# Value units ahead of logits, later x parts, own tiles for raw output weights, and VectorE remainders behind two sums, in a gated mix of attention and SwiGLU

## The chip, the cores and the metric

The kernel runs on one core of one Trainium2 chip. The metric is the device time of one execution in microseconds (us), lower is better. The engines are named as the profile names them: PE is TensorE's matmul, PEld its weight load, DVE is VectorE, ACT is ScalarE, POOL is GpSimd, SP is SyncE, which issues the DMAs.

## The reference

The input x has 2048 tokens of width 576. One branch is an attention with 32 heads of width 18 over four segments of 512 tokens with a memory carried from segment to segment; the other is a SwiGLU network of width 4608. A gate mixes the two.

```python
for s in range(N):                                    # N = 4 segments of L = 512
    qs, ks, vs = q[:, :, s], k[:, :, s], v[:, :, s]
    logits = jnp.einsum("bhqd,bhkd->bhqk", qs, ks) * scale + mask
    p = _softmax(logits, axis=-1)
    a_dot = jnp.einsum("bhqk,bhkd->bhqd", p, vs)
    pq = phi(qs)
    num = jnp.einsum("bhld,bhde->bhle", pq, M)
    den = jnp.einsum("bhld,bhd->bhl", pq, z)[..., None] + 1e-6
    outs.append(g * (num / den) + (1.0 - g) * a_dot)
    M = M + jnp.einsum("bhld,bhle->bhde", phi(ks), vs)
    z = z + jnp.einsum("bhld->bhd", phi(ks))
a = concat_heads(outs) @ wo
b = (_silu(x @ w_gate) * (x @ w_up)) @ w_down
out = sigmoid((x * gate_w).sum(-1)) * a + (1 - that gate) * b
```

The mask adds -1e9 where the key lies behind the query in the segment. Products with x, wq, wk, wv, wo, w_gate, w_up and w_down are in fp32.

## The kernel before

**Number format.** Most products are made from a high and a low half of each operand. The high half is a ScalarE copy, rounded; the low half is the remainder that VectorE subtracts (`low`, L271; `split_by`, L963; `split`, L137). Each product then takes hi·hi, hi·lo and lo·hi.

**First phase, up to about 220 us.** For each of the four segments the kernel makes queries and keys (`qk`), values (`v_step`, matmuls at L159), the update of the memory, and `mem_step` (L460), which reads the memory for 128 tokens and half of the heads. It runs 24 times, one call behind each value step of the segments 1 to 3, and takes PSUM banks 3, 4 and 2 in turn.

**Second phase, about 217 to 1635 us.** The hidden width is cut into 36 features of 128. The tokens are cut into two halves; features 0 to 35 in the text are those of the first half, 36 to 71 of the second. Gate and up projection of a feature are made together for two segments, with a scheme of seven products in place of eight (as Strassen's). `seven(t, j)` is product j, 0 to 6: six matmuls of 128x128 by 512 at L1018 and one at L1021 for the last 64 input rows. Products accumulate into three PSUM banks a, y and xx, with copies and sums between them: y = a + p5 (VectorE, L1087) must be done before product 5 adds to it; xx = copy of a (ScalarE, L1094) before product 6 adds to it; the sum p5 = a + p5 (VectorE, L1095) is used only in the closing multiplications (L1103, L1104). With q the number of the feature modulo 3, the features with q=0 also run the down projection of the three features before, in groups of nine matmuls (L868) whose results VectorE adds to `ya` (L876, L878).

**What sets the order.** The order in which the Python code calls the engines is the order in each engine's queue; the waits between engines follow from the tiles. Each feature has eight beats, k = 0 to 7, called between the products (`tick`, `beat`). A beat first issues what was deferred to it (`due`), then down groups, then, by a credit, a step of attention. Deferred are the preparation of the next feature's weights (`w_make`: sums on GpSimd, L264; high halves on ScalarE, L268; low halves on VectorE, L271; at the beats of the tables HIGH and LOW), the halves of the hidden values (`split_by`, L962 and L963) and of the down weights, and the loads. By these tables the low halves for products 4, 5 and 6 come up at the beats k = 1, 2 and 3 of the feature that uses them.

**Attention** is a generator, `att_gen`. Its step tau is the n-th, 0 to 5, of a unit of six. In a step with n from 0 to 4 it makes logits (`s_bank`, L726, into a bank that `ts_tile` gives), one step later the row maxima (VectorE, L732) and exponentials (ScalarE, L744), three steps later the cast to two 16-bit halves (L758 on VectorE, L759 on GpSimd), and four steps later the transposing DMA (SP, L763). After six steps a value unit is due (`v_unit`, matmuls at L774 and L775, a reduce at L781). `ts_tile` has banks 5 and 6 while down groups are pending, and one more rule: directly after a new set of groups came (`fed`), bank 7.

**The break.** Between features 35 and 36 ten beats (919 to 945 us) run the last 16 down groups' work and make the x operands of the second half (`x_second`): loads, sums on GpSimd and splits (L136 on ScalarE, L137 on VectorE), each at a beat that the tables LOADS, SUMS and PARTS name as (beat, z, j). **The end**: from feature 71 on the weights of the output projection are loaded (`wo_load`, L910) into the ring `raw` that also holds the feature weights, split (L913, L914), and used in a tail from about 1635 us on.

Of the kernel before, what the change touches and what calls it, by code (L numbers as in the profile page):

```python
# [12 lines left out]
F32 = mybir.dt.float32  # L13
# [7 lines left out]
P = 128  # L21
S = 2048
D = 576
# [4 lines left out]
FT = 36  # L28
# [4 lines left out]
NT = 5  # L33
HR = [(128 * t // DH, -(-min(128 * t + 128, D) // DH)) for t in range(NT)]
MW = max(b - a for a, b in HR) * E
CH = 3
# [12 lines left out]
SHARE = (0, 0, 2, 2, 3, 3, 3, 3)  # L49
BREAK = 10  # L50
LOADS = ((-3, 0, 0), (-2, 0, 1), (3, 1, 0), (4, 1, 3), (4, 0, 3), (5, 0, 2), (5, 1, 1), (6, 1, 2))
SUMS = ((2, 0, 1), (9, 0, 4), (10, 0, 2), (10, 1, 1), (11, 1, 4), (12, 0, 6), (12, 1, 2), (13, 1, 6))
PARTS = ((1, 0, 0), (4, 0, 1), (10, 1, 0), (10, 0, 5), (11, 0, 3), (11, 1, 5), (12, 1, 3), (13, 0, 4), (14, 0, 2),
         (14, 1, 1), (15, 1, 4), (16, 1, 2), (17, 0, 6), (18, 1, 6))
FIRST = (9, 10, 11, 15, 17, 17, 19)
SLOT = (0, 3, 2, 1, 4, 6, 5)
RPOS = (0, 1, 4, 2, 5, 6, 3)
# [4 lines left out]
def f32(ap):  # L62
    return ap.bitcast(F32)
# [3 lines left out]
def gated_mix(ctx, tc, xT, xrest, wf, wfr, wfh, wd, wv, wo, beta, cmask, ident, bmask, out):  # L67
    nc = tc.nc
# [44 lines left out]
    taken = {}  # L113
    clock = [0]
    fed = []
# [6 lines left out]

    def ts_tile(shape=(P, L)):
        ids = (5, 6) if groups else (5, 6, 7, 3, 4)
        if fed and groups[0][0] < FT // CH - 1 and max(taken, key=taken.get) != 7:
            ids = (7,)
        fed.clear()
        return ps.tile(list(shape), F32, name=f"bank{soonest(ids, HELD)}")

    def group_tile(shape=(P, L)):  # L130
        return ps.tile(list(shape), F32, name=f"bank{soonest((3, 4, 7), 1)}")

    groups = []

    def split(hi, lo, src):
        nc.scalar.activation(hi, src, AF.Copy)  # L136
# [79 lines left out]
    def raw_tile():  # L216
        return rp.tile([P, L], F32, name="raw")
# [14 lines left out]
    def op_tile():  # L232
        return wop.tile([P, 2, 2, P], F32R, name="wo_")
# [22 lines left out]
    def w_make(half, f, LOW=LOW):  # L256
        g, u = wraw_of.pop(f)
        ops = wops[half, f] = [None] * 7
        a11, a12, a21, a22 = g[:, 0:2], g[:, 2:4], u[:, 0:2], u[:, 2:4]
        src = [a11, None, None, a12, None, None, a22]  # L260

        def total(j, p, q, sub=True):
            src[j] = rp.tile([P, 2, P], F32, name="ws", bufs=3)
            (nc.gpsimd.tensor_sub if sub else nc.gpsimd.tensor_add)(src[j], p(), q())  # L264

        def high(j):
            ops[j] = op_tile()
            nc.scalar.activation(ops[j][:, 0], src[j], AF.Copy)  # L268

        def low(j):  # L270
            nc.vector.tensor_sub(ops[j][:, 1], src[j], f32(ops[j][:, 0]))  # L271

        def keep(j):
            nc.sync.dma_start(wc[f, j], f32(ops[j]).rearrange("p a k n -> p (a k n)"))

        todo = [(LEAD - 2, lambda: total(1, lambda: a21, lambda: a22, False)),
                (LEAD - 1, lambda: total(2, lambda: src[1], lambda: a11)),
                (LEAD + 2, lambda: total(4, lambda: a11, lambda: a21)),
                (LEAD + 4, lambda: total(5, lambda: a12, lambda: src[2]))]
        for j in range(7):  # L280
            todo += [(HIGH[j], lambda j=j: high(j)), (LOW[j], lambda j=j: low(j))]
            if half == 0 and f < KEPT:
                todo.append((LEAD + j + 3, lambda j=j: keep(j)))
        return sorted(todo, key=lambda t: t[0])
# [3 lines left out]
    with ExitStack() as st:  # L288
# [310 lines left out]
        for s in range(NSEG):  # L599
# [58 lines left out]
            for n in range(8):  # L658
                hf, i = divmod(n, 4)
                flush()  # L660
                v_step(s, hf, i)
                if s:
                    mem_step(s, n // 2, n % 2)
                if s < 3:
                    if n == 0:
                        xs_of[s + 1] = x_tiles(s + 1)
                    if 1 <= n < 6:
                        x_split(xs_of[s + 1], n - 1, raws["x", n - 1])
                else:
                    if n == 4:  # L670
                        wraw_of[1] = [w_load(1, u) for u in range(2)]
                    if n < 2:
                        first_sum(6, n)
                    elif n < 6:
                        if n < 4:
                            nc.gpsimd.memset(f32(rhs[n - 2][96:]), 0.0)
                        if 3 <= n < 5:
                            r_fetch(n - 3)
                    if n > 2:
                        for z in stack_loads(0)[2 * n - 6:2 * n - 4]:  # L680
                            nc.sync.dma_start(*z)
# [8 lines left out]
    with ExitStack() as st:  # L690
        cps = []
        due = deque()

        def defer(k, fn):
            while len(due) < k:
                due.append([])
            due[k - 1].append(fn)

        rw = pool(st, "rw", 4)
        fp = pool(st, "fp", CH)  # L700
# [97 lines left out]
        def att_gen():  # L798
            N = 12 * NB

            def at(t):
                return 5 * (t // 6) + t % 6 if 0 <= t < N and t % 6 < 5 else None

            held = []
            for tau in range(N + 10):
                u, n = divmod(tau, 6)
                if n == 2 and sends:
                    nc.sync.dma_start(*sends.pop(0))
                if 1 <= n <= 3 and u + 1 < 2 * NB:
                    for d in stack_loads(u + 1)[3 * n - 3:3 * n]:  # L810
                        nc.sync.dma_start(*d)
                if n == 2 and u > 1 and u % 2 == 1 and (u - 3) // 2 < NB:
                    o_step((u - 3) // 2)
                z = at(tau - PL)
                if z is not None:
                    p_bank(z)
                z = at(tau - 1)
                if z is not None:
                    e_bank(z)
                if n == 5 and 1 <= u <= 2 * NB:  # L820
                    held.append(u)
                if held and (groups or n == 0):
                    v = held.pop()
                    v_unit(v - 1)
                    if v % 4 == 1 and v // 4 + 1 < 4 * NSEG:
                        v_fetch(v // 4 + 1)
                z = at(tau)
                if z is not None:
                    s_bank(z)
                z = at(tau - XL)  # L830
                if z is not None:
                    x_bank(z)
                yield
            for z in sends:
                nc.sync.dma_start(*z)
# [10 lines left out]
        def d_fetch(f):  # L846
            d = d_tile()
            nc.sync.dma_start(f32(d).rearrange("p a n -> p (a n)"), dc[f])
            return d
# [50 lines left out]
        def gates():  # L900
            nc.vector.tensor_scalar_add(gg, gg, 1.0)
            nc.vector.reciprocal(gg, gg)
            nc.vector.tensor_scalar(g1, gg, -1.0, 1.0, op0=OP.mult, op1=OP.add)

        def wo_load(n, hf, c):
            box = []

            def load():
                box.append(raw_tile()[:, :96 * NT].rearrange("p (k n) -> p k n", n=96))
                nc.sync.dma_start(box[0], wo[:, :, 288 * hf + c.start:288 * hf + c.stop])  # L910

            defer(n, load)
            defer(n + 5, lambda: nc.scalar.activation(wos[hf][:, 0, :, c], box[0], AF.Copy))  # L913
            defer(n + 7, lambda: nc.vector.tensor_sub(wos[hf][:, 1, :, c], box[0], f32(wos[hf][:, 0, :, c])))  # L914
# [45 lines left out]

        def split_by(k, hi, lo, src):
            defer(k, lambda: nc.scalar.activation(hi, src, AF.Copy))  # L962
            defer(k + 1, lambda: nc.vector.tensor_sub(lo, src, f32(hi)))  # L963

        def beat(k=None, half=0):
            for fn in due.popleft() if due else ():
# [57 lines left out]
        draw = {}  # L1024
# [4 lines left out]
        for pos, (half, f) in enumerate(seq):  # L1029
# [27 lines left out]
            def tick():  # L1057
                k = step[0]
                step[0] += 1
                if k % 2 == 0 and f and stores:  # L1060
                    nc.sync.dma_start(*stores.pop(0))
                if half == 0:
                    if (q, k) in ((0, 3), (1, 3), (2, 2)):
                        draw[f] = d_load(f)
                    if (q, k) in ((1, 1), (1, 7), (2, 4)):
                        g = f - 1 if k == 1 else f
                        ds[half, g] = d_split(g, draw.pop(g))
                elif (q, k) in ((1, 0), (1, 2), (2, 1)):
                    g = f - 1 if k == 0 else f
                    ds[half, g] = d_fetch(g)  # L1070
                beat(k, half)

            ops, rem = wops.pop((half, f)), rhs[f % 2]
            hh = fp.tile([P, 2, L], F32R, name="hh")
# [10 lines left out]
            seven(a, 2, False)  # L1085
            y = y_tile()
            nc.vector.tensor_add(y, a, p5)  # L1087
            tick()
            seven(xx, 3, False)
            nc.scalar.activation(sg0, xx, AF.Copy)  # L1090
# [2 lines left out]
            xx = x_tile()  # L1093
            nc.scalar.activation(xx, a, AF.Copy)  # L1094
            nc.vector.tensor_add(p5, a, p5)  # L1095
            tick()
            nc.scalar.activation(sg0, sg0, AF.Silu)  # L1097
            seven(y, 5, False)
# [33 lines left out]
        ops = None  # L1132
# [6 lines left out]
        for n in range(17):  # L1139
# [24 lines left out]
            ops = nxt  # L1164
# [54 lines left out]
```

## Time and profile before

| | us |
|---|---|
| median of three runs (lowest to highest) | 1724.15 (1723.75 to 1724.97) |
| the profiled execution, its own time | 1724.43 |
| its span, first to last instruction | 1722.7 |
| TensorE busy | 1706.5 |
| VectorE busy | 1359.8 |
| ScalarE busy | 1084.8 |
| GpSimd busy | 938.4 |

The span is what lies between the first and the last instruction of the profiled execution; the rest of its time lies around it. A busy time counts an engine's instructions, and pipelined matmuls overlap: a row's length is longer than the distance to the next. In a timeline each row has a start, a length, the engine, the line, the operation, the tiles written and read, and a count for a run of like instructions; a bracket at its end gives the idle time before and what ended it. Granted clock was 1.000 of full speed.

### The profile page before, as it was taken

How to read it: one execution, taken by the hardware profiler on the slowest of the kernel's cores; microseconds unless marked ns; L12 is line 12 of the kernel's file. 1: busy time of each engine (PE TensorE's matmuls, PEld its weight loads, DVE VectorE, ACT ScalarE, POOL GpSimd, SP SyncE). 2: the span in 40 equal slices, each digit the busy share in tenths (PEclk: the TensorE clock that was granted, in tenths of full speed). 3: DMA queues.
4: the chain of work that ended last, by engine and by line, in shares of the span. 5: the costliest groups of instructions: out<-in, count | busy, mean ns of one | idle time of the engine just before them, and what ended most of it. 6: DMA issues, size and time to landing. Idle time of an engine off the chain costs nothing.

```text
span 1722.7 us, 34832 instructions
## 1 busy us (share of the span) xinstructions
PE 1706.5 (99%) x11868; PEld 1481.0 (86%) x11868; DVE 1359.8 (79%) x3231; ACT 1084.8 (63%) x2123; POOL 938.4 (54%) x1194
## 2 busy tenths in 40 slices
PE   9999999999999999999999999999999999999999
PEld 7899978888888888888887888888888888888899
DVE  6557588898899889898989677788887778778655
ACT  7666585776677577667765755765666576566411
POOL 4434646666666656565666555555555555555221
PEclk9999999999999999999999999999999999999999
DMA  8654499999998898988879986887778677767544
GB/s 284 233 186 153 151 311 191 232 226 186 209 227 192 181 215 200 193 198 203 210 144 256 290 177 133 178 186 162 148 181 182 147 157 185 163 132 167 165 144 137
DMA packets 524002, 328.05 MB, mean 190 GB/s; under 512 B 411184, under 2 KB 460336, under 8 KB 523824
## 3 DMA queue, kind: packets, MB, share of 16 engines
q1 hardware_dynamic: 523824, 325.83, 77.5%
q8 instruction: 93, 1.52, 0.4%
q14 instruction: 85, 0.70, 0.1%
HBM read 165.76 MB, written 76.09 MB: 140 GB/s over the span
## 4 chain that ended last, share of the span: by engine, by line
PE 83%; DVE 6%; ACT 5%; DMA 3%; issue 2%; POOL 1%; SPq 1%; DVEq 0%; ACTq 0%; POOLq 0%
PE bank L1018 33%; PE bank L868 24%; PE bank L159 10%; PE bank L1021 5%; PE bank L726 4%; PE bank L774 2%; PE bank L775 1%; PE bank L414 1%; ACT pe L744 1%; ACT L744 1%; PE bank L460 1%; DVE xo L137 1%; DVE p L758 1%; DVE scr L732 1%; PE bank L350 1%
## 5 line engine op out<-in xcount | busy, mean ns | idle before, releaser
L759 POOL TENSOR_TENSOR p<-pe,p 128x512 f16<-128x512 f32 x320 | 376.0, 1175 | 420.4 <-DVE p L758 406.2
L868 PE MATMUL bank<-dw,hh 128*128 128x320 f32 (+1 forms) x2304 | 489.0, 305 | 2.8 <-DVE ya L878 2.8
L868 PEld LDWEIGHTS bank<-dw,hh 128*128 128x128 f32 x2304 | 381.4, 190 | 14.4 <-DVE ya L878 3.8
L744 ACT ACTIVATE pe<-bank,mb 128x512 f32<-128x512 f32 (+3 forms) x512 | 247.9, 526 | 197.7 <-DVE mb L732 191.3
L868 PE MATMUL bank<-dw,hl 128*128 128x320 f32 (+1 forms) x1152 | 340.6, 296 | 0.2 <-DVE hl L137 0.2
L732 DVE CUSTOM_DVE_ANT_0 scr<-bank,cm 128x512 bf16<-128x512 f32 (+3 forms) x512 | 246.6, 482 | 6.8 <-PE bank L726 0.2
L878 DVE TENSOR_TENSOR ya<-bank,ya 128x320 f32<-128x320 f32 x352 | 158.3, 453 | 83.9 <-PE bank L868 83.2
L868 PEld LDWEIGHTS bank<-dw,hl 128*128 128x128 f32 x1152 | 218.0, 189 | 0.4 <-DVE hl L137 0.4
L1021 PE MATMUL bank<-xr,rh 128*128 128x512 f32 x504 | 196.5, 390 | 0.0
L752 POOL TENSOR_SCALAR_AFFINE_SELECT pe<-pe 128x256 f32<-128x256 f32 (+1 forms) x320 | 149.8, 469 | 54.1 <-ACT pe L744 51.0
L758 DVE CAST p<-pe 128x512 f16<-128x512 f32 x320 | 152.5, 477 | 0.0
L264 POOL TENSOR_TENSOR ws<-raw 128x256 f32<-128x256 f32 x140 | 118.3, 845 | 17.4 <-DMA raw<-in_wf_dram 4.5
L726 PE MATMUL bank<-kst,qst 108*128 108x512 bf16 (+3 forms) x512 | 125.2, 306 | 2.1 <-ACT pe L744 2.1
L1021 PEld LDWEIGHTS bank<-xr,rh 128*128 128x128 f32 x504 | 94.7, 188 | 20.3
L963 DVE TENSOR_TENSOR hl<-row,hh 128x512 fp32r<-128x512 f32 x120 | 104.2, 868 | 8.3 <-ACT hh L962 7.8
L1095 DVE TENSOR_TENSOR row<-bank,row 128x512 f32<-128x512 f32 x72 | 49.7, 690 | 64.7 <-ACT bank L1094 64.5
L744 ACT ACT_TABLE_LOAD x69 | 88.5, 1283 | 11.1 <-DVE mb L732 10.1
L1080 ACT ACTIVATE bank<-bank 128x512 f32<-128x512 f32 x72 | 41.9, 582 | 80.5 <-PE bank L1021 77.4
L1090 ACT ACTIVATE row<-bank 128x512 f32<-128x512 f32 x72 | 43.3, 601 | 78.0 <-PE bank L1021 77.8
L1097 ACT ACT_TABLE_LOAD x71 | 91.1, 1283 | 1.3
L264 POOL TENSOR_TENSOR ws<-raw,ws 128x256 f32<-128x256 f32 x70 | 58.3, 833 | 49.4 <-DVE wo__22504 L271 10.9
L159 PE MATMUL bank<-xo,qhi 128*128 128x512 f32 x264 | 83.2, 396 | 0.4 <-ACT vps L399 0.4
(2166 smaller groups left out, 4097.9 us busy)
## 6 DMA issues: line engine op xcount, KB each, us to landing
raw<-in_wf_dram SPq DMA_DIRECT2D x140, 256.0 KB
rh<-rc SPq DMA_DIRECT2D x72, 336.0 KB
dc<-dw SPq DMA_DIRECT2D x36, 576.0 KB
dw<-dc SPq DMA_DIRECT2D x36, 576.0 KB
stk<-q SPq DMA_DIRECT2D x32, 384.0 KB
draw<-in_wd_dram SPq DMA_DIRECT2D x36, 288.0 KB
rc<-rt SPq DMA_DIRECT2D x42, 224.0 KB
vd<-vps SPq DMA_DIRECT2D x8, 912.0 KB
```

The source lines that it names most:

```text
L159: nc.tensor.matmul(t, st[n], mv[n], start=(n == 0), stop=(n == 13))
L264: (nc.gpsimd.tensor_sub if sub else nc.gpsimd.tensor_add)(src[j], p(), q())
L726: nc.tensor.matmul(t[:, c:c + w], qs[:KR, pr, P * i:P * i + P], ks[:KR, pr, 0:w], start=True, stop=True)
L732: nc.vector.tensor_tensor_reduce(scr[:, :w], t[:, c:c + w], cm[:, L - w:L], -SCALE, 3.0e38, OP.add, OP.min, m[:, k:k + 1])
L744: nc.scalar.activation(pe[:, c:c + w], t[:, c:c + w], AF.Exp, bias=m[:, k:k + 1], scale=SCALE)
L752: nc.gpsimd.affine_select(d, d, pattern=pat, compare_op=OP.is_ge, fill=0.0, base=0, channel_multiplier=1)
L758: nc.vector.tensor_copy(p[:, 0], pe)
L759: nc.gpsimd.tensor_sub(p[:, 1], pe, p[:, 0])
L868: nc.tensor.matmul(ts[m], p, q[:, cs], start=(n == 0), stop=(n == 3 * CH - 1))
L878: nc.vector.tensor_add(ya[:, i, cs], t, ya[:, i, cs])
L1018: nc.tensor.matmul(t, w[:, p, z], x[z][:, q], start=first and n == 0, stop=False, skip_group_check=True)
L1021: nc.tensor.matmul(t, rem[:, RPOS[j]], XR[j], start=False, stop=True, skip_group_check=True)
```

## The change

There are six edits.

1. A value unit that is due is always issued in a step with n = 0, which has logits directly behind it. Before, it was issued at the next step whenever down groups were pending.
2. `ts_tile`'s rule for bank 7 applies to the logits alone, and no longer to the value unit's bank.
3. `mem_step` is called twice behind every second value step, not once behind each.
4. The x operands of the second half are split in another order and at later beats; three splits and one sum move behind the ten beats of the break, into feature 36.
5. The raw output weights have other tiles in three places: two of their own (`wr`) and the one of `draw`, which is free by then.
6. VectorE remainders (`low` and that of `split_by`) that come up in the beats k=1 and k=3 of a feature are held back, and issued directly behind the sum at L1087 (those of k=1) or the sum at L1095 (those of k=3).

```diff
-SUMS = ((2, 0, 1), (9, 0, 4), (10, 0, 2), (10, 1, 1), (11, 1, 4), (12, 0, 6), (12, 1, 2), (13, 1, 6))
+SUMS = ((2, 0, 1), (9, 0, 4), (10, 1, 1), (11, 1, 4), (12, 1, 2), (13, 1, 6), (14, 0, 2), (19, 0, 6))
...
-        if fed and groups[0][0] < FT // CH - 1 and max(taken, key=taken.get) != 7:
-            ids = (7,)
-        fed.clear()
+        if fed and len(shape) == 2:
+            if groups[0][0] < FT // CH - 1 and max(taken, key=taken.get) != 7:
+                ids = (7,)
+            fed.clear()
...
+    stash, holds = [], [False]
+
+    def behind(fn):
+        if holds[0]:
+            stash.append(fn)
+        else:
+            fn()
+
+    def let_go():
+        while stash:
+            stash.pop(0)()
...
         def low(j):
-            nc.vector.tensor_sub(ops[j][:, 1], src[j], f32(ops[j][:, 0]))
+            behind(lambda: nc.vector.tensor_sub(ops[j][:, 1], src[j], f32(ops[j][:, 0])))
...
-                if s:
-                    mem_step(s, n // 2, n % 2)
+                if s and n % 2:
+                    for bank in range(2):
+                        mem_step(s, n // 2, bank)
...
-                if held and (groups or n == 0):
+                if held and n == 0:
                     v = held.pop()
                     v_unit(v - 1)
...
+        def wo_home(n):
+            if n in (4, 5):
+                return cps[0].tile([P, 96 * NT], F32, name="wr", bufs=2)
+            if n == 8:
+                return fp.tile([P, D], F32, name="draw", bufs=1)[:, :96 * NT]
+            return raw_tile()[:, :96 * NT]
+
             def load():
-                box.append(raw_tile()[:, :96 * NT].rearrange("p (k n) -> p k n", n=96))
+                box.append(wo_home(n).rearrange("p (k n) -> p k n", n=96))
...
         def split_by(k, hi, lo, src):
             defer(k, lambda: nc.scalar.activation(hi, src, AF.Copy))
-            defer(k + 1, lambda: nc.vector.tensor_sub(lo, src, f32(hi)))
+            defer(k + 1, lambda: behind(lambda: nc.vector.tensor_sub(lo, src, f32(hi))))
...
+                holds[0] = k in (1, 3)
                 beat(k, half)
+                holds[0] = False
...
             nc.vector.tensor_add(y, a, p5)
+            let_go()
             tick()
...
             nc.vector.tensor_add(p5, a, p5)
+            let_go()
             tick()
```

In the changed file the lines have moved: the sum y is L1109, p5 L1118, the low remainder L283, that of `split_by` L983, products L1038 and L1041, logits L739, values L787 and L788, row maxima L745, the cast L771, down groups L881.

VectorE in feature 53, from the sum y (the first row) to behind the sum p5 (L1095 before, L1118 after); a number behind wo__ names one weight operand, of product 4 (17930), 5 (17949) or 6 (17963 before, 17962 after), and in the last row of before 18003 is product 0 of the next feature. Before:

```order
L1087 TENSOR_TENSOR bank_17997<-bank_17934,row 128x512
L271 TENSOR_TENSOR wo__17949<-ws,wo__17949 128x256
L963 TENSOR_TENSOR hl<-row,hh 128x512
L271 TENSOR_TENSOR wo__17963<-raw,wo__17963 128x256
L758 CAST p<-pe 128x512
L732 ISA scr,mb_2326<-bank_18029,cm 128x128
L732 ISA mb_2326 128x1
L732 ISA scr,mb_2326<-bank_18029,cm 128x384
L732 ISA mb_2326 128x1
L1095 TENSOR_TENSOR row<-bank_17934,row 128x512
L271 TENSOR_TENSOR wo__18003<-raw,wo__18003 128x256
```

After:

```order
L1109 TENSOR_TENSOR bank_17995<-bank_17934,row 128x512
L283 TENSOR_TENSOR wo__17930<-ws,wo__17930 128x256
L983 TENSOR_TENSOR hl<-row,hh 128x512
L283 TENSOR_TENSOR wo__17949<-ws,wo__17949 128x256
L983 TENSOR_TENSOR hl<-row,hh 128x512
L771 CAST p<-pe 128x512
L745 ISA scr,mb_2326<-bank_18028,cm 128x128
L745 ISA mb_2326 128x1
L745 ISA scr,mb_2326<-bank_18028,cm 128x384
L745 ISA mb_2326 128x1
L1118 TENSOR_TENSOR row<-bank_17934,row 128x512
L283 TENSOR_TENSOR wo__17962<-raw,wo__17962 128x256
```

The remainder of product 4 and one of the hidden values, ahead of y before, stand behind it now, and the remainder of product 6 has moved from ahead of the row maxima to behind p5.

TensorE in feature 30, the end of a value unit and what follows. Before, the unit stands between two products:

```order
L774 LDWEIGHTS pt
L774 MATMUL bank_11257<-v,pt 128x57
L775 LDWEIGHTS pt
L775 MATMUL bank_11257<-v,pt 128x38
L1018 MATMUL bank_11198<-xo_2273,wo__11132 128x512 x3
L1018 MATMUL bank_11198<-xo_2304,wo__11132 128x512 x3
L1021 MATMUL bank_11198<-xr_1662,rh_2331 128x512
L868 MATMUL bank_11323<-dw,hh 128x320 x2
```

After, logits stand directly behind the unit, and down groups behind those:

```order
L787 LDWEIGHTS pt
L787 MATMUL bank_11294<-v,pt 128x57
L788 LDWEIGHTS pt
L788 MATMUL bank_11294<-v,pt 128x38
L739 LDWEIGHTS qst_2321
L739 MATMUL bank_11337<-kst_2322,qst_2321 128x512
L881 MATMUL bank_11343<-dw,hh 128x256 x2
L881 MATMUL bank_11343<-dw,hl 128x256
```

The unit has moved down by a product and a part of the down groups, to the next step with n = 0.

More of the change, by code (lines that the diff above doesn't have):

```diff
@@ L51 @@
 LOADS = ((-3, 0, 0), (-2, 0, 1), (3, 1, 0), (4, 1, 3), (4, 0, 3), (5, 0, 2), (5, 1, 1), (6, 1, 2))
-SUMS = ((2, 0, 1), (9, 0, 4), (10, 0, 2), (10, 1, 1), (11, 1, 4), (12, 0, 6), (12, 1, 2), (13, 1, 6))
-PARTS = ((1, 0, 0), (4, 0, 1), (10, 1, 0), (10, 0, 5), (11, 0, 3), (11, 1, 5), (12, 1, 3), (13, 0, 4), (14, 0, 2),
-         (14, 1, 1), (15, 1, 4), (16, 1, 2), (17, 0, 6), (18, 1, 6))
+SUMS = ((2, 0, 1), (9, 0, 4), (10, 1, 1), (11, 1, 4), (12, 1, 2), (13, 1, 6), (14, 0, 2), (19, 0, 6))
+PARTS = ((1, 0, 0), (4, 0, 1), (10, 1, 0), (11, 1, 5), (12, 1, 3), (13, 0, 5), (13, 1, 1), (14, 1, 4), (15, 1, 2),
+         (17, 0, 2), (17, 1, 6), (18, 0, 3), (20, 0, 4), (22, 0, 6))
 FIRST = (9, 10, 11, 15, 17, 17, 19)
```

## The prediction

> **What bounds the kernel now.** I read the page first, then the list of waits, then the timelines around the places the change touches. The page gives the span, the busy time of each engine, and the share of each engine in the chain that ended last.
>
> ```profile
> span 1722.7 us, 34832 instructions
> PE 1706.5 (99%) x11868; PEld 1481.0 (86%) x11868; DVE 1359.8 (79%) x3231; ACT 1084.8 (63%) x2123; POOL 938.4 (54%) x1194
> PE 83%; DVE 6%; ACT 5%; DMA 3%; issue 2%; POOL 1%; SPq 1%; DVEq 0%; ACTq 0%; POOLq 0%
> ```
>
> TensorE is busy 99% of the span and the diff takes no matmul away. So only three things can move the time: gaps on TensorE, what a matmul loses when the kind of product changes, and waits put in new. The list of waits (microseconds in total, times, longest) has those at lines the change touches:
>
> ```profile
> PEld bank L1018 <- ACT bank L1094: 8.0, 11, 1.9
> PE bank L1018 <- DVE bank L1087: 1.1, 2, 0.7
> PEld bank L1018 <- DVE bank L1087: 3.5, 7, 1.1
> PE bank L868 <- DVE ya L878: 2.8, 4, 0.9
> PE bank L726 <- ACT pe L744: 2.1, 6, 0.4
> DVE row L1095 <- ACT bank L1094: 64.5, 57, 2.8
> SPq L763 <- PE bank L775: 28.0, 19, 4.1
> ```
>
> **What the change gives.** *Value units ahead of logits.* In timelines a row gives its start and its length, and x6 is a run of six matmuls. Here is a value unit alone between two products of seven, a logits matmul alone, and the two one behind the other:
>
> ```profile
> 801.77 0.40 PE L1021 MATMUL bank<-xr,rh 128*128 128x512 f32 x1
> 802.01 0.20 PE L774 MATMUL bank<-v,pt 128*128 128x57 bf16 x1
> 803.07 1.63 PE L1018 MATMUL bank<-xo,wo__11132 128*128 128x512 f32 x6
> ...
> 381.75 0.39 PE L1021 MATMUL bank<-xr,rh 128*128 128x512 f32 x1
> 382.02 1.74 PE L1018 MATMUL bank<-xo,wo__4804 128*128 128x512 f32 x6
> ...
> 840.04 0.39 PE L1021 MATMUL bank<-xr,rh 128*128 128x512 f32 x1
> 841.32 0.38 PE L726 MATMUL bank<-kst,qst 108*128 108x512 bf16 x1
> 841.35 1.76 PE L1018 MATMUL bank<-xo,wo__11672 128*128 128x512 f32 x6
> ...
> 1274.46 1.52 PE L1018 MATMUL bank<-xo,wo__17949 128*128 128x512 f32 x6
> 1276.05 1.61 PE L1018 MATMUL bank<-xo,wo__17963 128*128 128x512 f32 x6
> ```
>
> Two products in a row start 1276.05−1274.46 = 1.59 apart, which is seven matmuls of 0.23, and an undisturbed run of six takes 1.52. The unit alone costs 803.07−801.77−0.23 = 1.07, and 1.63−1.52 = 0.11 more in the run behind it: 1.18. Logits alone cost 0.04+0.22 = 0.26. Both together cost 1.08+0.24 = 1.32, against 1.44 apart, so a joining saves 0.12. In the order of the instructions 25 of the 64 units already stood ahead of a logits matmul and 37 more now do: −4.4.
>
> *Logits' bank.* Units now leave bank 7 to the logits. Six times logits waited for the exponential on the bank of earlier ones (the fifth row of the waits). One of them, the down group's matmul and then the logits:
>
> ```profile
> 385.00 0.31 PE L868 MATMUL bank<-dw,hl 128*128 128x320 f32 x1
> 385.66 0.38 PE L726 MATMUL bank<-kst,qst 108*128 108x128 bf16 x2 [0.35 <-ACT pe L744]
> ```
>
> A 320-column matmul has a pitch of 0.15 (the same 0.23 for 512 columns, scaled), so 385.66−385.00−0.15 = 0.51 is lost; six times, −3.1.
>
> *Memory steps in pairs.* A memory step makes the twelve value projections behind it 1.83 long where they are 1.74 undisturbed. Twelve fewer returns: 12×0.09 = −1.1.
>
> ```profile
> 87.32 1.74 PE L159 MATMUL bank<-vw,xo 128*128 128x288 f32 x12
> 89.82 1.83 PE L159 MATMUL bank<-vw,xo 128*128 128x288 f32 x12
> ```
>
> *Output weights.* In feature 71 ScalarE waits 2.50 us for a raw load (L913), which makes its copy L1094 late, on which the seventh product starts:
>
> ```profile
> 1626.69 0.61 ACT L913 ACTIVATE wo<-raw 128x480 fp32r<-128x480 f32 x1 [2.50 <-DMA raw<-in_wo_dram]
> 1628.65 0.39 PE L1021 MATMUL bank<-xr,rh 128*128 128x512 f32 x1
> 1630.47 0.96 PE L1018 MATMUL bank<-xo,wo__22927 128*128 128x512 f32 x3 [1.43 <-ACT bank L1094]
> ```
>
> With tiles of their own the loads need not wait for readers of the ring, and SP issues them some microseconds earlier. The gap is 1630.47−1628.65−0.23 = 1.59: −1.5.
>
> *The break.* VectorE is busy 25.69 of the 26 us between the halves, and TensorE only 22.82 (columns: TensorE, its loads, VectorE, ScalarE, GpSimd, then clock, DMA share, GB/s):
>
> ```profile
> 919.00:945.00 26.00, 22.82 (x194) 21.11 (x193) 25.69 (x47) 13.18 (x25) 19.39 (x17) 1.00 1.12 285
> 930.53 1.77 DVE L137 TENSOR_TENSOR xo<-wo__12935,xo 128x512 fp32r<-128x512 f32 x1
> 942.59 0.68 DVE L137 TENSOR_TENSOR xo<-wo__12970,xo 128x512 fp32r<-128x512 f32 x1
> ```
>
> Three of twelve x remainders, about 0.9 each, go to feature 36: −2.7 here. One of them stands behind its p5 sum, wanted by the seventh product: +0.6. Net −2.1.
>
> *The sum y.* Product 5 accumulates onto y = a + p5 (L1087). Seven times its weights waited for it; three of these cost the matmuls more than 0.06 (0.52, 0.29 and the 0.87 below, 913.75−912.66−0.23). Now two remainders stand behind y, not ahead of it: −1.7. The bounds are the 1.1 and the 3.5 of the two rows at L1087.
>
> ```profile
> 912.66 0.39 PE L1021 MATMUL bank<-xr,rh 128*128 128x512 f32 x1
> 913.75 0.50 PE L1018 MATMUL bank<-xo,wo__12823 128*128 128x512 f32 x1 [0.71 <-DVE bank L1087]
> ```
>
> The gains come to −13.9; with the smaller ones at half it is −9, with all of the 3.5 at L1087 about −16.
>
> **What it costs.** *The low remainder behind p5.* By the new order the remainder held back at k=3 is the low half of the weights of the seventh product, j=6, and that product's third matmul loads it. Ahead of it now stands the sum p5 (L1095), which no product needs soon and which waits for ScalarE's copy L1094 in 57 of 72 features. That is a new wait on the path. No row of before shows it, but another remainder stands at the same place there and gives the times. First a feature in which L1094 is late (53), then an ordinary one (40):
>
> ```profile
> 1275.98 0.69 DVE L1095 TENSOR_TENSOR row<-bank,row 128x512 f32<-128x512 f32 x1 [1.49 <-ACT bank L1094]
> 1276.59 0.42 DVE L271 TENSOR_TENSOR wo__18003<-raw,wo__18003 128x256 fp32r<-128x256 f32 x1
> ...
> 1026.88 0.42 DVE L271 TENSOR_TENSOR wo__14411<-raw,wo__14411 128x256 fp32r<-128x256 f32 x1
> 1027.01 1.52 PE L1018 MATMUL bank<-xo,wo__14380 128*128 128x512 f32 x6
> ```
>
> In feature 53 the product started at 1276.05 (above), its third matmul two pitches later, at 1276.50. The remainder will end at 1276.59+0.42 = 1277.01: 0.5 late, 0.6 with the 0.11 that the first matmul after a wait takes longer (0.50 above against 0.39). The eleven waits for L1094 less the one of feature 71 are ten such features; where the remainder is itself slowed (next row) they pay 1.1. I take 0.8: **+8.0**. In feature 40 the remainder ends at 1027.30 and the matmul wants it at 1027.46, but its weight load must run before that. So it is at the margin: 0 to 0.5, and I take 0.2, nearer to this row. Features with q=0 (every third) have down groups between the products and pay nothing; 38 others remain: **+7.6**.
>
> *Slowed remainders.* Beside a GpSimd sum a remainder takes 0.91, not 0.42:
>
> ```profile
> 797.31 0.75 POOL L264 TENSOR_TENSOR ws<-raw 128x256 f32<-128x256 f32 x1
> 797.43 0.91 DVE L271 TENSOR_TENSOR wo__11116<-raw,wo__11116 128x256 fp32r<-128x256 f32 x1
> ```
>
> The Trainium skill, page "SBUF — State Buffer", section "SBUF: two separate sides", calls the port pair that VectorE and GpSimd share an exclusive lock: the loser blocks for the whole instruction. These rows agree in part, since 0.91 is less than the 0.42 and the 0.75 together.
>
> *Product 4 and the exponentials.* At k=1 a low remainder and an hl remainder move behind y. Where y waits with VectorE idle (features 1 and 11), they push the row maxima, the exponentials and so the copy L1094 back. In feature 11 y waits idle behind this pair:
>
> ```profile
> 430.58 0.68 DVE L963 TENSOR_TENSOR hl<-row,hh 128x512 fp32r<-128x512 f32 x1
> 431.76 0.70 DVE L1087 TENSOR_TENSOR bank<-bank,row 128x512 f32<-128x512 f32 x1 [0.50 <-ACT row L1083]
> ```
>
> Starts lie 0.33 behind a lone remainder and 0.60 behind the hl one: 0.93, in two features: **+1.9**. Elsewhere VectorE has the time before product 4.
>
> *Costed at nothing.* SP's transposes already wait for value units (the last row of the waits) and will do so about sixty times; the products that read them come four steps of attention later, some microseconds, which hides it. If that cover were gone, the loads queued behind them on SP would be late next, and a step's 0.7 at L868 is the nearest price. The second memory step of a pair has its drain on VectorE as before, with three banks in turn. The sum (19,0,6) is GpSimd's, which is busy 54%.
>
> **The sum.** −13.9 + 8.0 + 7.6 + 1.9 = +3.6. The profiled execution took 1724.43 (its span and 1.7 around it), 0.28 above the median of the runs: 1724.4 + 3.6 − 0.3 = **1727.7**, slower by 0.2%, which is about what a measurement of this kernel can tell from no change.
>
> **Rivals.** *The remainder is in time.* This ends on the other side. In the features other than the ten the margin of 0.16 holds, and the ten pay 0.5 each: 1724.4 − 13.9 + 5.0 − 0.3 = 1715.2. For it speaks that 1027.30 lies ahead of 1027.46; against it that the load comes before the matmul. It decides the sign where the mean price over the 48 features is below 13.9/48 = 0.29 us.
>
> *Collisions.* GpSimd stands beside most remainders behind p5. At 0.91 each is 0.49 longer: the 38 are then 0.33 late, 0.44 with the restart, and the ten pay 0.49 more: +9.1 + 4.9, 1742. Against it: in feature 40 it takes 0.42. By the skill's lock, "SBUF — State Buffer", it would be 0.42+0.75 = 1.17 at every one, and 0.70 for each of the 38; that would give an estimate of 1754, but the row of 0.91 is nearer.
>
> *Units and logits joined stall what follows.* Behind them a down group's bank would wait for ya, 0.7 a time (2.8 over 4). If 12 of the 37 do: +8.4, 1736. For it: VectorE has the reduce of the unit and the maxima of the logits at once. Against it: that wait is now rare, and 25 joined units live well.
>
> **How the numbers follow.** The forecast has 0.47, with a range of its own from 1719 to 1740 (prices 0 to 0.5 in the 38, gains 9 to 16). In time has 0.30 (1713 to 1718), collisions 0.13 (1742 to 1754), joined stalls 0.10 (1733 to 1739). The range 1713 to 1742 leaves out most of the collisions and little else. Faster than no change: 0.27 of the in-time case and 0.05 of the forecast's lower end, 0.32. Slower: 0.28 of the forecast and both other rivals, 0.51, and 0.01 of the in-time case: 0.52. The same: 0.16.
>
> **What would show it.** In the waits after: a wait of TensorE's weight loads for the weight remainder, absent before, with its count over 20 and a total near 10 if I am right, or ten short ones if the in-time rival is. The six waits of logits for the exponential, the 1.43 near the end, and the y waits should be gone, and the break's TensorE share higher. A unit standing apart from its logits, or a break as idle as before, would make the gains wrong. Remainders behind p5 with a mean near 0.9 would show collisions.

## The result and the profile after

The changed kernel takes 1748.21 us (median of 4 runs, 1746.41 to 1749.16) where the kernel before, run beside it, takes 1724.41. The ratio is 1.0132, with a 95% interval from 1.0119 to 1.0145: slower by 23.8 us. The direction was forecast, the size was not: +3.6 was expected, and 1748.21 lies above the range.

The page of the profile after, its span and the busy time of each engine:

```profile
span 1745.7 us, 34856 instructions
PE 1718.4 (98%) x11868; PEld 1476.2 (85%) x11868; DVE 1349.8 (77%) x3231; ACT 1085.0 (62%) x2123; POOL 934.3 (54%) x1194
```

No engine has more instructions in its row. VectorE is busy 10 us less than before in a span that is 23 us longer, so it idles 33 us more. VectorE's waits for its sum y before the change (L1087), and then from the list of waits after, VectorE's and TensorE's:

```profile
DVE bank L1087 <- PE bank L1021: 12.5, 21, 1.6
DVE bank L1087 <- ACT row L1083: 11.4, 12, 1.8
DVE bank L1087 <- ACT hh L962: 1.9, 4, 1.3
...
DVE row L1118 <- ACT bank L1117: 52.1, 43, 1.9
DVE bank L1109 <- PE bank L1041: 38.4, 32, 4.1
DVE bank L1109 <- ACT row L1105: 29.7, 14, 3.3
DVE bank L1109 <- ACT hh L982: 7.6, 4, 2.4
...
PE bank L1038 <- ACT bank L1117: 5.5, 8, 1.7
PE bank L881 <- DVE ya L891: 1.4, 5, 0.4
PE bank L1038 <- DVE wo__3681 L283: 0.9, 1, 0.9
PE bank L1038 <- DVE wo__9081 L283: 0.8, 1, 0.8
PE bank L1038 <- DVE wo__11788 L283: 0.8, 1, 0.8
```

L1109 is the sum y and L1118 the sum p5. Ahead of y VectorE now idles 75.7 us in 50 features (the three rows at L1109), against 25.8 us in 37 before the change. TensorE has the new wait that was forecast: for weight remainders (L283), one row for each weight tile since each has its own name. All such rows together are 11.3 us in 24 waits of matmuls, and 33.3 us in 60 waits of the weight loads ahead of them. The six waits of logits for the exponential are gone.

Counted from the start of each matmul to the start of the next, and summed, the six matmuls of the products at L1038 take about 25.5 us more than before, and all else together about 2.5 us less. Of the 25.5, about 20 lie ahead of the third and fourth matmul of product 6, and about 3 ahead of those two of product 0: the places where the low half of the weights is loaded.

Feature 31 after the change shows how it comes about. VectorE first, then ScalarE's copy, then TensorE at product 6:

```profile
855.20 0.70 DVE L1109 TENSOR_TENSOR bank<-bank,row 128x512 f32<-128x512 f32 x1 [1.74 <-ACT hh L982]
855.81 0.41 DVE L283 TENSOR_TENSOR wo__11672<-ws,wo__11672 128x256 fp32r<-128x256 f32 x1
856.14 0.69 DVE L983 TENSOR_TENSOR hl<-row,hh 128x512 fp32r<-128x512 f32 x1
...
860.10 0.68 DVE L745 CUSTOM_DVE_ANT_0 scr<-bank,cm 128x512 bf16<-128x512 f32 x1
860.71 0.69 DVE L1118 TENSOR_TENSOR row<-bank,row 128x512 f32<-128x512 f32 x1
861.31 1.13 DVE L283 TENSOR_TENSOR wo__11788<-raw,wo__11788 128x256 fp32r<-128x256 f32 x1
...
859.69 0.58 ACT L1117 ACTIVATE bank<-bank 128x512 f32<-128x512 f32 x1 [1.76 <-PE bank L1041]
...
861.03 0.61 PE L1038 MATMUL bank<-xo,wo__11788 128*128 128x512 f32 x2
862.49 1.20 PE L1038 MATMUL bank<-xo,wo__11788 128*128 128x512 f32 x4 [0.84 <-DVE wo__11788 L283]
```

VectorE idles 1.74 us ahead of y while the two remainders that it could have made meanwhile stand behind y. It then works without a pause up to p5, which starts at 860.71 although the copy it needs was done at 859.69+0.58 = 860.27. So VectorE comes late to p5 (with the hold at k=3 alone, told below, it is early in this feature and waits 0.51 us for the copy). The weight remainder ends at 862.44, and the third matmul, wanted at 861.03+0.45 = 861.48, starts at 862.49. The remainder is a long one here, 1.13; with 0.42 it would have ended at 861.73 and still have been late, by 0.25.

### The profile page after: what moved, and what is told of

The parts are those of the page before. It is cut to its first block, busy times and chain, and to the rows that moved or that the text cites. A ratio compares the mean times of both kernels' runs of the same rounds, so it can differ in the third digit from the quotient of the medians.

```text
span 1745.7 us, 34856 instructions
## 1 busy us (share of the span) xinstructions
PE 1718.4 (98%) x11868; PEld 1476.2 (85%) x11868; DVE 1349.8 (77%) x3231; ACT 1085.0 (62%) x2123; POOL 934.3 (54%) x1194
## 5 line engine op out<-in xcount | busy, mean ns | idle before, releaser
L881 PE MATMUL bank<-dw,hh 128*128 128x320 f32 (+1 forms) x2304 | 487.4, 304 | 1.4 <-DVE ya L891 1.4
L881 PEld LDWEIGHTS bank<-dw,hh 128*128 128x128 f32 x2304 | 380.9, 189 | 14.4 <-DVE ya L891 3.7
L881 PE MATMUL bank<-dw,hl 128*128 128x320 f32 (+1 forms) x1152 | 340.6, 296 | 1.4 <-DVE hl L149 1.4
L745 DVE CUSTOM_DVE_ANT_0 scr<-bank,cm 128x512 bf16<-128x512 f32 (+3 forms) x512 | 246.8, 482 | 13.9 <-PE bank L739 6.9
L881 PEld LDWEIGHTS bank<-dw,hl 128*128 128x128 f32 x1152 | 217.9, 189 | 1.9 <-DVE hl L149 1.9
L1041 PE MATMUL bank<-xr,rh 128*128 128x512 f32 x504 | 196.7, 390 | 0.0
L765 POOL TENSOR_SCALAR_AFFINE_SELECT pe<-pe 128x256 f32<-128x256 f32 (+1 forms) x320 | 145.4, 455 | 64.5 <-ACT pe L757 56.9
L771 DVE CAST p<-pe 128x512 f16<-128x512 f32 x320 | 157.8, 495 | 0.0
L739 PE MATMUL bank<-kst,qst 108*128 108x512 bf16 (+3 forms) x512 | 124.6, 305 | 0.0
L276 POOL TENSOR_TENSOR ws<-raw 128x256 f32<-128x256 f32 x140 | 113.8, 813 | 11.2 <-DMA raw<-in_wf_dram 7.9
L1041 PEld LDWEIGHTS bank<-xr,rh 128*128 128x128 f32 x504 | 94.8, 188 | 20.8
L1109 DVE TENSOR_TENSOR bank<-bank,row 128x512 f32<-128x512 f32 x72 | 50.3, 699 | 76.4 <-PE bank L1041 38.4
L983 DVE TENSOR_TENSOR hl<-row,hh 128x512 fp32r<-128x512 f32 x120 | 96.7, 807 | 0.0
L276 POOL TENSOR_TENSOR ws<-ws,raw 128x256 f32<-128x256 f32 x70 | 70.1, 1002 | 44.5 <-POOL ws L276 5.9
L1118 DVE TENSOR_TENSOR row<-bank,row 128x512 f32<-128x512 f32 x72 | 49.6, 689 | 52.3 <-ACT bank L1117 52.1
L1113 ACT ACTIVATE row<-bank 128x512 f32<-128x512 f32 x72 | 43.2, 601 | 71.7 <-PE bank L1041 71.6
```

What stands on the lines that cost most here:

```text
L739: nc.tensor.matmul(t[:, c:c + w], qs[:KR, pr, P * i:P * i + P], ks[:KR, pr, 0:w], start=True, stop=True)
L745: nc.vector.tensor_tensor_reduce(scr[:, :w], t[:, c:c + w], cm[:, L - w:L], -SCALE, 3.0e38, OP.add, OP.min, m[:, k:k + 1])
L765: nc.gpsimd.affine_select(d, d, pattern=pat, compare_op=OP.is_ge, fill=0.0, base=0, channel_multiplier=1)
L771: nc.vector.tensor_copy(p[:, 0], pe)
L881: nc.tensor.matmul(ts[m], p, q[:, cs], start=(n == 0), stop=(n == 3 * CH - 1))
L983: defer(k + 1, lambda: behind(lambda: nc.vector.tensor_sub(lo, src, f32(hi))))
```

## The experiments

The kernel before was run beside each group; its median there was 1725.58 in the first, 1725.41 in the second, and 1724.78 in the third. Differences across groups carry this drift of up to 0.8 us. The groups are the three sections below, except that the first kernel of the third section ran in the second group.

### Which of the two holds costs

Three kernels differ from the changed one in edit 6, and one from the kernel before. With no remainder held:

```diff
-                holds[0] = k in (1, 3)
+                holds[0] = False
```

> The changed kernel with no remainder held back (edit 6 undone, the other five kept). In the changed trace product 6 waits for its own low remainder for about 21 us in all, and product 0 for about 3.5 us more than before. Theory (the remainder behind p5 is the loss): these go, 1716 to 1725 us. Rival (units joined to logits, or another of the five, is the loss): 1735 us or more. Rival (the hold at k=1 is the loss): 1716 to 1725 too; the next kernel tells that apart.

Measured: 1721.17 us, ratio 0.9975 (0.9964 to 0.9985). The five other edits together are faster than the kernel before by 4.4 us, and the holds cost 27. The rival that one of the five is the loss falls.

The hold at k=1 alone:

```diff
-                holds[0] = k in (1, 3)
+                holds[0] = k == 1
```

> The changed kernel with the hold at k=1 alone (behind y), none at k=3. Theory (the remainder behind p5 is the loss): within 2 us of the kernel without any hold. Rival (the hold at k=1 pushes maxima, exponentials and copies back): 10 us or more above it.

Measured: 1736.21 us, ratio 1.0063 (1.0050 to 1.0075), 15.0 above the kernel with no hold. My theory, that the place behind p5 is the loss, was wrong by more than half of it: the rival had the price right. Its way was wrong in part, though: the copies come late, but most of the loss lies elsewhere. The waits of VectorE, first with no hold and then with the hold at k=1:

```profile
DVE row L1118 <- ACT bank L1117: 63.0, 57, 2.3
DVE bank L1109 <- ACT row L1105: 11.5, 12, 1.8
DVE bank L1109 <- PE bank L1041: 11.3, 20, 1.6
DVE bank L1109 <- ACT hh L982: 1.9, 4, 1.3
```

```profile
DVE row L1118 <- ACT bank L1117: 37.0, 33, 1.9
DVE bank L1109 <- PE bank L1041: 35.8, 29, 4.1
DVE bank L1109 <- ACT row L1105: 27.9, 14, 3.3
DVE bank L1109 <- ACT hh L982: 5.2, 3, 1.7
DVE bank L1109 <- PE bank L739: 2.7, 1, 2.7
```

VectorE's idle time moves from behind its work to ahead of it: at y it grows by about 47 us, at p5 it shrinks by 26. TensorE pays where VectorE has run out of slack. In the sums over matmul starts product 0 waits about 7 us more for its low weights and product 6 about 4 more; the late copies L1117 add about 2 (TensorE's wait for them goes from 2.9 to 4.7). The few us that remain are spread over other places.

What is held at k=3, put ahead of p5 and not behind it (with the hold at k=1 kept):

```diff
-            nc.vector.tensor_add(p5, a, p5)
             let_go()
+            nc.vector.tensor_add(p5, a, p5)
```

> The changed kernel with what is held at k=3 issued directly ahead of the sum p5, not behind it. It is then still behind the row maxima, but not behind p5's 0.7 us and p5's wait for ScalarE's copy. Theory: most of the waits of product 6 go, 3 to 6 us above the kernel with the hold at k=1 alone (1726 to 1734). Rival (the maxima and the cast ahead of it, or collisions with GpSimd, make it late): 1738 us or more.

Measured: 1736.17 us, ratio 1.0066 (1.0052 to 1.0079), the same as with the hold at k=1 alone. So standing behind the row maxima costs nothing that shows, and all that the second hold adds, 12.0 us, comes from standing behind p5. The level is above what I expected since the hold at k=1 costs what I had not seen.

The hold at k=3 alone, in the kernel before (`holds[0] = k in (3,)`, with the stash and its release):

> The kernel before with the hold at k=3 alone, behind p5. Theory: it loses by itself what the whole change loses and somewhat more, since the gains are not there: 1744 to 1752 us. Rival (the loss needs the joined units, which fill VectorE at that place): 1736 us or less.

Measured: 1738.38 us, ratio 1.0071 (1.0059 to 1.0084): +12.8. Neither range holds it; the rival's lies nearer, but not for its reason, since the loss is there without any joined units. The two holds cost 12 to 13 and 15, and 27 together.

In this kernel the sum p5 is L1109 and the copy L1108:

```profile
DVE row L1109 <- ACT bank L1108: 86.2, 70, 2.8
```

VectorE waits for the copy in 70 of 72 features: it is early everywhere. Of the 48 features with q other than 0, product 6 waits some 0.5 to 1.1 us each in those whose copy is late, and next to nothing in the rest: 8.6 us in the 47 whose p5 starts as the copy ends. In the changed kernel only 24 of the 48 are of that kind, with the same 8.6 us between them, and in the 24 others VectorE comes to p5 after the copy's end, as in feature 31; these pay 11.2 more. Of these 20 us at product 6, about 4 are there with the hold at k=1 alone, and about 4 come off at product 0 when the second hold is added: that leaves the 12.0.

### What makes the hold at k=1 dear

Each half of what is held at k=1 was held alone, with nothing held at k=3. First the weight remainder (`split_by` without `behind`), then the remainder of the hidden values (`low` without `behind`):

```diff
-            defer(k + 1, lambda: behind(lambda: nc.vector.tensor_sub(lo, src, f32(hi))))
+            defer(k + 1, lambda: nc.vector.tensor_sub(lo, src, f32(hi)))
```

> The changed kernel with the weight remainder of product 4 alone held behind y (k=1); the remainder of the hidden values and those at k=3 are issued as before. With no hold the time was 1721.2, with both held at k=1 1736.2 us. Theory (VectorE idles ahead of y while the held work stands behind it, and what it does later, the weight remainders of the products 6 and 0, comes late): the loss goes with the work that is held, 0.33 of 0.93 us: 1724 to 1728. Rival (the pair's place matters by the one remainder that someone waits for, the weights' or the hidden values'): all of the loss, 1734 or more, or none, under 1723.

Measured: 1725.13 us, ratio 0.9999 (0.9990 to 1.0007); 3.9 above the kernel with no hold, as the theory had it.

```diff
-            behind(lambda: nc.vector.tensor_sub(ops[j][:, 1], src[j], f32(ops[j][:, 0])))
+            nc.vector.tensor_sub(ops[j][:, 1], src[j], f32(ops[j][:, 0]))
```

> The same with the remainder of the hidden values alone held behind y at k=1. Theory (loss by held work, 0.60 of 0.93 us): 1729 to 1733. Rival: under 1723, or 1734 or more.

Measured: 1727.48 us, ratio 1.0011 (1.0002 to 1.0019); 6.3 above no hold, below the theory's range and in neither of the rival's. By the order in the traces the weight remainder is held in 70 features, but that of the hidden values in 48 only, which the expectation did not reckon with. Both halves cost, the larger one more, and together they cost more (15.0) than apart (10.2). Idle time ahead of y goes with it: 24.7 us with no hold, 34.6 and 53.2 with the one and the other half, 71.6 with both.

The last of the group moves no remainder. It adds one VectorE instruction behind y in each feature:

```diff
             nc.vector.tensor_add(y, a, p5)
+            nc.vector.tensor_tensor(p5, p5, p5, op=OP.max)
```

> The changed kernel with no hold, and one more VectorE instruction in each feature directly behind y: the maximum of p5 with itself, 128x512, about 0.6 us that change no value. No remainder is moved. Theory (what counts is the VectorE time that is lost at this place, about 0.65 us a feature by the waits ahead of y): 1731 to 1741. Rival (the remainders' order itself counts, not the time): under 1725.

Measured: 1741.15 us, ratio 1.0089 (1.0076 to 1.0103), 20.0 above no hold. VectorE's busy time in its page:

```profile
PE 1711.1 (98%) x11868; PEld 1477.4 (85%) x11868; DVE 1420.4 (82%) x3303; ACT 1087.4 (63%) x2123; POOL 945.9 (54%) x1194
```

With no hold it is 1362.4, so 58 us more of VectorE work (0.8 for each, not 0.6), in a kernel that leaves VectorE idle a fifth of the time, lengthen the run by 20, the upper end of what the theory gave: 0.34 for each us. The hold at k=1 gives 15.0 for about 47 us more idle time ahead of y: 0.32. Its halves alone give 0.39 (3.9 for 9.9) and 0.22 (6.3 for 28.5), so a third is a rough price. In both, VectorE's wait at p5 shrinks alike, from 63.0 to 37.0 with the hold and to 35.3 with the extra instruction. TensorE pays in other places, though. With the hold about 11 of its 15 us lie ahead of the third and fourth matmuls of the products 0 and 6; with the extra instruction about 7 of its 20 do, and 8 lie ahead of the down groups, whose banks wait for the sums `ya`. The waits at p5 with the extra instruction, then at the down groups with no hold, with the hold at k=1 and with the extra instruction:

```profile
DVE row L1119 <- ACT bank L1118: 35.3, 36, 2.1
...
PE bank L881 <- DVE ya L891: 1.5, 5, 0.5
...
PE bank L881 <- DVE ya L891: 1.4, 5, 0.5
...
PE bank L881 <- DVE ya L891: 6.3, 12, 1.1
```

So it is shown that VectorE time lost behind y costs TensorE about a third of it, with no remainder moved. That the hold at k=1 costs by this lateness follows from the waits and the places in its own trace; the like price alone would not prove it, since the extra instruction's lateness arrives partly elsewhere. What it is not is an order that someone waits for directly: product 4, whose remainder was moved, does not wait for it (less than 1 us in all).

### The other edits, one by one

From the kernel with no hold, memory steps one by one again:

```diff
-                if s and n % 2:
-                    for bank in range(2):
-                        mem_step(s, n // 2, bank)
+                if s:
+                    mem_step(s, n // 2, n % 2)
```

> The changed kernel with no hold and the memory steps one by one, as before (edit 3 undone as well). The prediction had the pairs save 1.1 us: 1722.3. In the trace of the kernel without a hold the features 0 and 1 start 0.4 and 1.4 later than before, which is put down to the pairs: 1719 to 1720.

Measured: 1718.10 us, ratio 0.9958 (0.9945 to 0.9970): 3.1 faster than with pairs. That is below both expectations. This kernel, with the edits 1, 2, 4 and 5 alone, beats both the kernel before and the changed one. The start of the second phase with pairs (kernel with no hold), then with single steps, where the products are L1037 and L1040:

```profile
219.96 1.66 PE L472 MATMUL bank<-Mm,ph 128*128 128x152 f32 x12
224.45 0.39 PE L1041 MATMUL bank<-xr,rh 128*128 128x512 f32 x1
225.62 1.66 PE L1038 MATMUL bank<-xo,wo__2473 128*128 128x512 f32 x6 [0.78 <-ACT bank L1102]
```

```profile
223.58 0.39 PE L1040 MATMUL bank<-xr,rh 128*128 128x512 f32 x1
223.81 1.52 PE L1037 MATMUL bank<-xo,wo__2473 128*128 128x512 f32 x6
```

With pairs the third product of feature 0 starts 225.62−224.45−0.23 = 0.94 late, waiting for a ScalarE copy; with single steps it doesn't wait. That the last pair's work on VectorE holds the copy up is argued from its place, not shown. In the trace another 0.9 us stands already at the first product; the two traces are 2.1 us apart in all.

From that kernel, value units as before:

```diff
-                if held and n == 0:
+                if held and (groups or n == 0):
```

> The edits 2, 4 and 5 alone: no hold, single memory steps, and value units issued as before, at the next step whenever down groups are pending. With edit 1 the time was 1718.1. The prediction had the 37 joinings save 4.4 us: 1722.5. By the trace of the kernel without a hold they save some 1.5: 1719 to 1720.5. Rival (joined stalls): under 1718.

Measured: 1722.04 us, ratio 0.9986 (0.9978 to 0.9995). The joinings save 3.9 us, and the forecast of 4.4 was near; my reading of the first trace, 1.5, was too low. The rival of joined stalls falls.

The x operand (0,6) one beat earlier:

```diff
-         (17, 0, 2), (17, 1, 6), (18, 0, 3), (20, 0, 4), (22, 0, 6))
+         (17, 0, 2), (17, 1, 6), (18, 0, 3), (20, 0, 4), (21, 0, 6))
```

> The edits 1, 2, 4 and 5, with the x operand (0,6) split one beat earlier in feature 36, ahead of the sum p5. In the kernel with these edits feature 36 and the next take 1.1 us longer than before. If the place behind p5 costs that, as the prediction had it (0.6): 1717.0 to 1717.6. If other work of feature 36 does: 1718.1.

Measured: 1718.87 us (1717.12 to 1720.63), ratio 0.9964 (0.9952 to 0.9977): not told apart from the 1718.10. In its trace feature 36 is 0.54 shorter, as the place behind p5 would have it, but the first phase is 2.1 longer, which this edit doesn't touch. The runs leave it open.

The tables of the break as before:

```diff
-SUMS = ((2, 0, 1), (9, 0, 4), (10, 1, 1), (11, 1, 4), (12, 1, 2), (13, 1, 6), (14, 0, 2), (19, 0, 6))
+SUMS = ((2, 0, 1), (9, 0, 4), (10, 0, 2), (10, 1, 1), (11, 1, 4), (12, 0, 6), (12, 1, 2), (13, 1, 6))
```

(and PARTS as before)

> The edits 1, 2 and 5 alone: tables of the break as before. With the new tables 1718.1. The prediction had them save 2.1: 1720.2. By the trace, 2.2 in the break less 1.1 in feature 36: 1719.2.

Measured: 1719.67 us, ratio 0.9968 (0.9955 to 0.9980): the new tables save 1.6, between the two expectations and no better told apart than that. In the traces the stretch from the start of the last matmul of feature 35 to that of the first of feature 36 shrinks from 26.46 to 24.05, and feature 36 grows by 1.1.

The last kernel moves the multiplication of p5 from VectorE to GpSimd:

```diff
-            nc.vector.tensor_mul(sg1, p5, sg1)
+            nc.gpsimd.tensor_mul(sg1, p5, sg1)
```

> The edits 1, 2, 4 and 5, with the multiplication p5 by sg1 (0.6 us of VectorE in each feature) on GpSimd. Theory (VectorE time has the price that the extra instruction showed, 20 us for 43): freed, it gives at most what is left of waits for VectorE, 2 to 5 us: 1713 to 1716. Rival (VectorE has time to spare when nothing is held, and GpSimd is slower at it, so that the remainder of the hidden values and what follows comes late): 1718 or more.

Measured: 1734.15 us, ratio 1.0052 (1.0038 to 1.0066): 16 slower, as the rival had the sign. (The 43 us of the theory come from 0.6 for each extra instruction; by the pages it was 58.) What the traces show of it is told in the last section.

## Why the prediction was wrong, step by step

The runs put about 19 us between the sum of the forecast and the sum of what its parts measured. The hold at k=1 with what it does for the sum y was forecast at +0.2 and measured +15.0; the five other edits were forecast at −12.2 and measured −4.4; the hold at k=3 was forecast at +15.6 and added 12.0, which hides some 4 us of the rest.

- **The step that failed: the hold at k=1** ("Elsewhere VectorE has the time before product 4", +1.9 in two features). It measured +15.0. The step looked for someone who waits for the two remainders directly, found product 4 with time to spare, and stopped there. It also counted two features in which y waits with VectorE idle, where the list of waits before the change has 37 (21, 12 and 4 at L1087). The work that used to go ahead of that wait now adds to what follows. With this hold alone, what came late was the low half for product 6 (about 4 us) and, most of all, for product 0 of the next feature (about 7): no term of the prediction priced those.
- **The remainder behind p5: mechanism right, total near, shares wrong.** Forecast +15.6 (8.0 in the late features and 7.6 in the 38 others). Alone it measured +12.8, its waits by the trace 8.6 in late features and almost none elsewhere: there the in-time rival was right about the 38. On top of the hold at k=1 it added 12.0, since with VectorE behind, 24 of the other features paid 11.2 us. "In feature 40 ... it is at the margin" was true of a VectorE on time.
- **The collisions rival** was not what happened. Of the 34 remainders behind p5 that TensorE waited for, 4 took longer than 0.7 us, and their mean was 0.53, not 0.91. Had none taken more than 0.42, some 16 of the 20 us at these matmuls would remain, by an estimate from their rows. The rival's 1.17 adds two lengths in full, though in the rows shown for it the GpSimd sum had started 0.12 ahead and the remainder ended at 798.34, only 0.28 behind the sum's end at 798.06. That row is no evidence against a remainder that waits for the whole sum.
- **The joined stalls** did not come: waits at L881 for ya are 1.4 us after, less than the 2.8 before. SP's waits for value units grew (57.0 us in 41 waits, where about sixty were forecast, from 28.0 in 19), and no product shows a wait for it, as forecast.
- **The gains were oversized.** Joinings: 4.4 forecast, 3.9 measured. Break: 2.1 forecast, 1.6 measured. Memory pairs: 1.1 gained was forecast, 3.1 lost was measured; the step counted only the twelve returns to the value products, and not what the second step of a pair does to the start of feature 0. The bank rule and the output weights (3.1 and 1.5 forecast) are what is left of the five edits: 1 to 2 together, by which of the runs are subtracted. They were not run apart. By the trace the wait near the end is gone (1.6 us) and so are the six waits for the exponential, but TensorE has new waits ahead of down groups of about 0.35 us in feature 24 and in 27.
- **The sum y.** The wait for y that edit 6 removes was worth 1.7 in the forecast, which laid it to product 5. In the trace before, counted product by product, all seven waits stand ahead of product 4: it adds to the bank a, which y reads, and wo__12823 is its operand. The size was near all the same: the weight loads' wait there fell from 3.5 to 1.3 us. It was bought with the 15 of the hold at k=1.

## What to carry to other kernels

An engine that takes its work in the order of the program, as VectorE does here, and idles a fifth of its time may still have no time to give: what counts is whether its work stands ahead of its waits or behind them. Before work is put behind an instruction, look at how long the engine waits ahead of that instruction: the part of the wait that the work used to fill becomes a delay for all that follows, and its price can show a product or a feature later, at an operand that nobody moved. Where two edits eat the same engine's slack, cost the second with the first in place: here the total came out near the sum of the two apart (27.0, from 12.8 and 15.0), but other features and another product paid it.

## What the runs showed that was not expected

Moving 72 multiplications from VectorE to GpSimd made VectorE busier, not less busy. The pages of the kernel with the edits 1, 2, 4 and 5, then of the same with the move:

```profile
PE 1702.5 (99%) x11868; PEld 1479.4 (86%) x11868; DVE 1361.5 (79%) x3231; ACT 1085.8 (63%) x2123; POOL 939.5 (55%) x1194
```

```profile
PE 1710.4 (99%) x11868; PEld 1479.9 (85%) x11868; DVE 1379.8 (80%) x3159; ACT 1089.1 (63%) x2123; POOL 1037.6 (60%) x1266
```

The multiplications that left VectorE had been 59.0 us of its busy time, by the view of groups of the former kernel (busy us, mean ns, idle before):

```profile
L1127 DVE TENSOR_TENSOR row<-row 128x512 f32<-128x512 f32 x72 | 59.0, 819 | 0.0
```

So the instructions that stayed took 1379.8−(1361.5−59.0) = 77 us longer, beside 98 us more of GpSimd. Summed over the rows of the traces, 60 of these lie in the 490 weight remainders, whose mean goes from 0.59 to 0.72 us. The Trainium skill, page "SBUF — State Buffer", section "SBUF: two separate sides", says that VectorE and GpSimd share a port pair that one of them holds for a whole instruction. The two pages of the profile above agree in direction; that the port is the cause was not tested apart. Nor do the runs tell apart how much of the 16 us comes from slower VectorE work, and how much from the multiplication itself, which ends 0.4 us later on GpSimd (median, behind product 6) and holds up the hidden values: VectorE's waits for their high halves at L148 grow from 11.1 to 21.7 us. In the trace about 6 of the 16 lie ahead of product 4, where the wait for y grew, and 4.5 ahead of the down groups.
